# The second K/V unit's V issued before its K and the next query load, in a grouped-query attention kernel on one core

## Chip, core and metric

One core of one Trainium2 chip. The metric is the device time of the whole program in microseconds (us), lower is better.

## What is computed

```python
B, Hq, Hkv, Sq, Sk, D = 16, 32, 8, 288, 512, 128      # bf16
k, v = repeat(k, Hq // Hkv), repeat(v, Hq // Hkv)      # along the heads
p = softmax(einsum("bhqd,bhkd->bhqk", q, k) * D ** -0.5)
out = einsum("bhqk,bhkd->bhqd", p, v)
```

## The kernel before

There are 128 groups (one K/V head of one batch each), and three steps in a group, 384 in all. A step is three score matmuls of 128x512 on TensorE into PSUM, one exponential over 128x1536 on ScalarE, and twelve 128x129 products with V on TensorE; VectorE normalizes and evicts. In every sixth step VectorE computes 120 columns of the exponential itself (y_sb, t_sb, m_sb, e_sb, u_sb). I call it a shared step; a narrow 128x120 score matmul marks it. Steps 6, 12 and 18 are the first three.

K and V are loaded by units of four groups: K and Q by a transposing DMA, V by a plain one into vd_sb, all issued by SyncE in a fixed order. GpSimd copies V of one group at a time from vd_sb into v_sb. "Unit 1" is groups 4 to 7; K1 and V1 are its loads, Q4 is the query load of group 4. Step 12 is the first step of group 4.

```python
def op_v(u, eng=None, g0=0, g1=UG):                    # plain load, 512 KB for a unit
    ...
    eng.dma_start(vd_sb[:, sl, g0:g1], v_v[:, u * UG + g0:u * UG + g1]
                  ).then_inc(sem["us_v%d" % sl if u > 0 else "s_v%d" % g0], 16)

def op_s(n):                                           # scores of step n
    g, i = n // NC, n % NC                             # NC = 3 steps in a group
    waits = [have("k", g), have_q(g, i)]
    ...

def op_vc(g):                                          # V copy of group g, on GpSimd
    waits = [have("v", g)]
    if g >= 2:
        waits.append(("s_pv", NC * (g - 2) + 2))       # so many product groups are done
    ...

# the order of SyncE's issues is a sort by keys, in steps:
for u in range(1, NU):
    t = max(NC * UG * (u - NSLOT + 1) + 0.5, NC * (UG * u - 2.5) / AHEAD - 0.2)
    sp.append((t, lambda u=u: op_k(u)))
    sp.append((t + (2.0 if u >= NSLOT else 0.35), lambda u=u: op_v(u)))
for g in range(UG, NG):
    t = max(NC * (g - NQ + 1) + 1.2, NC * (g - 2.5) / AHEAD)
    sp.append((t, lambda g=g: op_q(g)))
...
sp.sort(key=lambda x: x[0])
```

## Time and profile before

| | before |
|---|---|
| median of 3 runs | 521.99 us (521.82 to 522.11) |
| traced run, span | 520.2 us |
| one step, steady | 1.330 us |
| K1, Q4, V1 landed | 18.0, 18.9, 21.9 us |
| score matmuls of step 12 start | 20.20 us |

A timeline line gives the start, the length, the engine, the source line, the operation, output and input, and, in square brackets, idle time of the engine before it and what ended that. A line of the DMA view gives the load, its issuing queue and the time from issue to landing, so a landing is the issue's start plus that number. Lines of the profile name source lines of the kernel: L449 is the score matmul, L460 the narrow one, L489 the product with V, L578 the V copy, L543 and L550 VectorE's t_sb and m_sb/e_sb.

### The profile page before, as it was taken

How to read it: one execution, taken by the hardware profiler on the slowest of the kernel's cores; microseconds unless marked ns; L12 is line 12 of the kernel's file. 1: busy time of each engine (PE TensorE's matmuls, PEld its weight loads, DVE VectorE, ACT ScalarE, POOL GpSimd, SP SyncE). 2: the span in 40 equal slices, each digit the busy share in tenths (PEclk: the TensorE clock that was granted, in tenths of full speed). 3: DMA queues.
4: the chain of work that ended last, by engine and by line, in shares of the span. 5: the costliest groups of instructions: out<-in, count | busy, mean ns of one | idle time of the engine just before them, and what ended most of it. 6: DMA issues, size and time to landing. Idle time of an engine off the chain costs nothing.

```text
span 520.2 us, 15366 instructions
## 1 busy us (share of the span) xinstructions
PE 516.2 (99%) x6226; PEld 394.6 (76%) x6226; DVE 370.5 (71%) x1322; ACT 513.4 (99%) x393; POOL 79.8 (15%) x135
## 2 busy tenths in 40 slices
PE   9999999999999999999999999999999999999997
PEld 5777777777777777777777777777777777777776
DVE  2767767777777677676776776767767767777777
ACT  7999999999999999999999999999999999999997
POOL 1111111111111111111111111111111111111110
PEclk9999999999999999999999999999999999999999
DMA  8999999899999998999999999999999999998212
GB/s 167 211 234 269 257 206 250 213 205 223 212 228 263 220 240 203 225 240 240 223 235 211 201 235 215 246 191 190 230 241 238 230 205 184 198 216 221 84 69 93
DMA packets 253782, 110.06 MB, mean 212 GB/s; under 512 B 220304, under 2 KB 237584, under 8 KB 253712
## 3 DMA queue, kind: packets, MB, share of 16 engines
q1 hardware_dynamic: 253568, 108.95, 99.5%
q8 instruction: 49, 0.80, 0.7%
q14 instruction: 21, 0.17, 0.1%
q10 hardware_dynamic: 144, 0.13, 0.1%
HBM read 16.91 MB, written 37.75 MB: 105 GB/s over the span
## 4 chain that ended last, share of the span: by engine, by line
PE 97%; DVE 2%; ACT 1%; issue 0%
PE ps_o L489 49%; PE ps_s L449 46%; PE ps_o L460 1%; ACT pt_sb L521 1%; ACT pt_sb L526 1%; PE ps_o L427 0%; DVE o_sb L595 0%; DVE u_sb L559 0%; DVE rl_sb L585 0%; DVE m_sb L550 0%; PE ps_s L427 0%; DVE pt_sb L566 0%; PE ps_o L414 0%; DVE t_sb L543 0%; DVE o_sb L605 0%
## 5 line engine op out<-in xcount | busy, mean ns | idle before, releaser
L526 ACT ACTIVATE pt_sb<-ps_s 128x1536 bf16<-128x1536 f32 (+2 forms) x384 | 508.2, 1438 | 0.1
L489 PE MATMUL ps_o<-v_sb,pt_sb 128*128 128x129 bf16 x4584 | 322.6, 220 | 0.1
L489 PEld LDWEIGHTS ps_o<-v_sb,pt_sb 128*128 128x128 bf16 x4584 | 282.6, 98 | 50.2 <-DVE o_sb L595 14.1
L449 PE MATMUL ps_s<-qt_sb,kt_sb 128*128 128x512 bf16 (+2 forms) x1536 | 308.9, 324 | 0.2
L595 DVE TENSOR_TENSOR o_sb<-ps_o,rl_sb 128x384 bf16<-128x384 f32 x382 | 211.7, 554 | 8.8
L449 PEld LDWEIGHTS ps_s<-qt_sb,kt_sb 128*128 128x128 bf16 x1536 | 123.6, 98 | 61.9 <-ACT pt_sb L526 0.7
L585 DVE RECIPROCAL rl_sb<-ps_o 128x3 f32<-128x3 f32 x382 | 67.8, 178 | 128.6 <-PE ps_o L489 127.2
L578 POOL COPY v_sb<-vd_sb 128x512 bf16<-128x512 bf16 x128 | 78.8, 616 | 429.2 <-PE ps_o L489 407.6
L559 DVE SCALAR_TENSOR_TENSOR u_sb<-u_sb,m_sb 128x120 f32<-128x120 f32 x128 | 36.2, 283 | 2.2
L566 DVE SCALAR_TENSOR_TENSOR pt_sb<-u_sb,e_sb 128x120 bf16<-128x120 f32 x64 | 18.1, 283 | 2.3
L559 DVE SCALAR_TENSOR_TENSOR u_sb<-m_sb 128x120 f32<-128x120 f32 x64 | 17.7, 276 | 0.0
L537 DVE TENSOR_SCALAR y_sb<-ps_o 128x120 f32<-128x120 f32 x64 | 16.2, 253 | 0.0
L550 DVE TENSOR_SCALAR m_sb<-t_sb 128x120 int32<-128x120 int32 x64 | 14.6, 228 | 2.2
L460 PE MATMUL ps_o<-qt_sb,kt_sb 128*128 128x120 bf16 x64 | 13.8, 216 | 0.0
L550 DVE TENSOR_SCALAR e_sb<-t_sb 128x120 int32<-128x120 int32 x64 | 13.8, 216 | 0.0
L543 DVE TENSOR_SCALAR t_sb<-y_sb 128x120 int32<-128x120 f32 x64 | 13.7, 214 | 0.0
L460 PEld LDWEIGHTS ps_o<-qt_sb,kt_sb 128*128 128x128 bf16 x64 | 6.3, 98 | 7.7 <-DVE o_sb L595 0.3
L521 ACT ACTIVATE pt_sb<-ps_s 128x512 bf16<-128x512 f32 (+1 forms) x6 | 4.3, 748 | 2.1 <-PE ps_s L449 2.1
L621 DVE TENSOR_REDUCE st_sb<-rl_sb 128x1 f32<-128x72 f32 (+1 forms) x16 | 3.4, 215 | 0.0
L623 DVE TENSOR_REDUCE st_sb<-rl_sb 128x1 f32<-128x72 f32 (+1 forms) x16 | 3.4, 215 | 0.0
L427 PE MATMUL ps_o<-const-bfloat16-1.0 128*128 128x512 bf16 (+1 forms) x6 | 2.4, 573 | 0.9 <-PEq L756 0.9
L685 ACT ACT_TABLE_LOAD x1 | 1.3, 1283 | 1.2 <-PEq L756 1.2
(32 smaller groups left out, 11.7 us busy)
## 6 DMA issues: line engine op xcount, KB each, us to landing
out_dram<-o_sb SPq DMA_DIRECT2D x126, 288.0 KB, 4.0
vd_sb<-in_v_dram SPq DMA_DIRECT2D x31, 512.0 KB, 5.4
qt_sb<-in_q_dram SPq DMA_TRANSPOSE x128, 5.1
out_dram<-o_sb SPq DMA_DIRECT2D x6, 96.0 KB, 1.8
kt_sb<-in_k_dram SPq DMA_TRANSPOSE x33, 5.1
vd_sb<-in_v_dram SPq DMA_DIRECT2D x2, 128.0 KB, 3.0
vd_sb<-in_v_dram SPq DMA_DIRECT2D x1, 256.0 KB, 3.5
kd_sb<-in_k_dram ACTq DMA_DIRECT2D x1, 128.0 KB, 2.3
```

Of the source, the lines that this page charges most:

```text
L449: ins = emit(eng, w_x, lambda: eng.matmul(ps_s[:, n % 2, c:c + w], kt_sb[:, sl, j, gi, :], qg[:, t * P:t * P + w], start=True, stop=True))
L460: emit(eng, [("s_ev", n - LAG - 1)], lambda: eng.matmul(ps_o[:, (n - LAG) % 2, BANK - W:BANK], kt_sb[:, (g // UG) % NSLOT, j, g % UG, :], ...
L489: ins = emit(eng, w_x, lambda: eng.matmul(outs(r)[:, t - r % NC * TPC, :], pt(g, t, j), v_sb[:, sl, gi * NJ + j, 0:DV], start=(x == 0), st ...
L526: emit(eng, waits, lambda: eng.activation(d, s, ACTF.Exp, scale=scale)).then_inc(sem["s_e"], 1)
L537: emit(eng, [("s_yb", nth(n) - NB), ("s_pv", n - LAG + 1)], lambda: eng.tensor_scalar(out=y_sb[:, b], in0=ps_o[:, (n - LAG) % 2, BANK - W: ...
L543: emit(eng, [("s_ym", 2 * (nth(n) - NB)), ("s_y", nth(n))], lambda: eng.tensor_scalar(out=t_sb[:, b], in0=y_sb[:, b], scalar1=Y_MUL, scala ...
L550: emit(eng, [("s_yp", nth(n) - NB), ("s_yb", nth(n))], lambda: eng.tensor_scalar(out=dst[:, b], in0=t_sb[:, b], scalar1=mask, scalar2=bits ...
L559: lambda: eng.scalar_tensor_tensor(out=u_sb[:, b, x], in0=src, scalar=QUARTIC[x], in1=m, op0=ALU.add, op1=ALU.mult)
L566: lambda: eng.scalar_tensor_tensor(out=pt_sb[:, n % NPT, CH - W:CH], in0=u_sb[:, b, 2], scalar=QUARTIC[3], in1=e_sb[:, b].bitcast(FP32), o ...
L578: emit(eng, waits, lambda: eng.tensor_copy(v_sb[:, sl, gi * NJ:(gi + 1) * NJ, 0:D], vd_sb[:, sl, gi].rearrange("p (j d) -> p j d", d=D))). ...
L585: emit(eng, [("s_pv", r + 1)], lambda: eng.reciprocal(rl_sb[:, TPC * r:TPC * (r + 1)].unsqueeze(2), outs(r)[:, :, D:DV])).then_inc(sem["s_ ...
L595: emit(eng, waits, lambda: eng.tensor_tensor(out=o_sb[:, g % NO, t0:t0 + TPC, :], in0=outs(r)[:, :, 0:D], in1=rl_sb[:, TPC * r:TPC * (r + ...
```

## The change

The intent: V of the second unit comes late (GpSimd waits 7.7 us for it), so it is asked for ahead of that unit's K and of the next query load. One sort key moves, and with it one issue; every engine but SyncE has the same instructions in the same order.

```diff
-            sp.append((t + (2.0 if u >= NSLOT else 0.35), lambda u=u: op_v(u)))
+            sp.append((t + (2.0 if u >= NSLOT else -0.05 if u == 1 else 0.35), lambda u=u: op_v(u)))
```

SyncE's order before is Q3, K1, Q4, V1, store 0, Q5; after, Q3, V1, K1, Q4, store 0, Q5.

## The prediction

> **What bounds the kernel now.** I read the page of the profiled execution first: its busy shares and its groups.
>
> ```profile
> span 520.2 us, 15366 instructions
> PE 516.2 (99%) x6226; PEld 394.6 (76%) x6226; DVE 370.5 (71%) x1322; ACT 513.4 (99%) x393; POOL 79.8 (15%) x135
> ...
> L526 ACT ACTIVATE pt_sb<-ps_s 128x1536 bf16<-128x1536 f32 (+2 forms) x384 | 508.2, 1438 | 0.1
> L489 PE MATMUL ps_o<-v_sb,pt_sb 128*128 128x129 bf16 x4584 | 322.6, 220 | 0.1
> ```
>
> TensorE and ScalarE are both busy 99% of the span, in lockstep: 384 steps, each of three 128x512 score matmuls, one exponential and twelve products with V. The chain of waits gives TensorE 97% of what ended last. The pace comes from the list of V copies on GpSimd, one per group of three steps: they start at 26.04 us (group 6) and at 509.00 us (group 127), so 482.96 us for 121 groups, 3.991 us a group, 1.330 us a step. The starts between go by the same 3.99 us (except one, at 34.50, whose V was late, and which moves none of those after it). So from 26 us on there is no slack that a load could give back; whatever a reordered load is worth must lie before 26 us. There, in the waits between 20 and 28 us, stand two that concern the moved transfer:
>
> ```profile
> POOL v_sb L578 <- DMA vd_sb<-in_v_dram: 7.7, 1, 7.7
> ...
> PEld ps_o L489 <- DVE o_sb L595: 0.6, 1, 0.6
> ```
>
> GpSimd waited 7.7 us for V from memory, and once the weight load of a product with V waited 0.6 us, the longest wait of its kind (the 62 of the whole run sum to 14.1 us). The chain in the same stretch (start, length, what) shows where it left TensorE:
>
> ```profile
> 21.02 0.69 PE ps_o L489 x12
> ...
> 22.08 0.47 DVE o_sb L595
> 22.55 0.23 DVE t_sb L543
> ...
> 22.80 0.52 DVE m_sb L550
> ...
> 25.12 0.85 PE ps_o L489 x12
> 25.97 0.65 PE ps_s L449 x3
> ```
>
> Between 21.71 and 25.12 us the end hangs on VectorE. The TensorE timeline has product groups starting at 22.18, 23.52, 25.12, 26.45 and 27.79 us: four intervals near 1.33 us except one, 23.52 to 25.12, which is 1.60. So 0.27 us is lost there. Why VectorE was late, by its own timeline (start, length) in this shared step and in the next one like it, eight microseconds later:
>
> ```profile
> 22.46 0.30 DVE L543 TENSOR_SCALAR t_sb<-y_sb 128x120 int32<-128x120 f32 x1
> 22.80 0.52 DVE L550 TENSOR_SCALAR m_sb<-t_sb 128x120 int32<-128x120 int32 x1
> ...
> 30.73 0.21 DVE L543 TENSOR_SCALAR t_sb<-y_sb 128x120 int32<-128x120 f32 x1
> 30.98 0.22 DVE L550 TENSOR_SCALAR m_sb<-t_sb 128x120 int32<-128x120 int32 x1
> ```
>
> The same instructions took 0.30 and 0.52 us instead of 0.21 and 0.22. GpSimd's timeline beside them:
>
> ```profile
> 22.07 1.17 POOL L578 COPY v_sb<-vd_sb 128x512 bf16<-128x512 bf16 x2 [7.68 <-DMA vd_sb<-in_v_dram]
> 26.04 0.62 POOL L578 COPY v_sb<-vd_sb 128x512 bf16<-128x512 bf16 x1 [2.79 <-PE ps_o L489]
> 30.03 0.62 POOL L578 COPY v_sb<-vd_sb 128x512 bf16<-128x512 bf16 x1 [3.38 <-PE ps_o L489]
> ```
>
> V of the second unit landed so late that the copies of groups 4 and 5 ran back to back, 22.07 to 23.24 us, across both slow instructions. Near 30 us one copy ran, 30.03 to 30.65, and VectorE's int32 work began at 30.73, just after it.
>
> **What the Trainium skill says.** "SBUF — State Buffer", the section with the two sides of SBUF and its diagram: VectorE and GpSimd share one port pair under an exclusive lock; a VectorE instruction in a 2-port mode, or with two SBUF inputs against a GpSimd read, and a GpSimd instruction exclude each other for a whole instruction. "VectorE: DVE Perf Modes", What auto-detection actually checks: the two-port mode needs a single source and the destination in SBUF. t_sb and m_sb are such; y_sb and the eviction, which read PSUM, are not. The trace agrees: the first end near the copies' ends, the others keep their 0.25 and 0.55 us beside a copy. "DMA: Bandwidth & Descriptors", Queues, rings and completion order: on each DMA engine descriptors are consumed in ring order. The landings below agree: they come in the order of issue.
>
> **The change part by part.** Nothing is added or removed; one issue moves. For the unit u=1 the sort key of V goes from 4.32 to 3.92, below K's 3.97 and Q4's 4.17. Old order on SyncE: K1, Q4, V1, store 0; new: V1, K1, Q4, store 0. No other key changes. The SyncE timeline has K1 issued at 11.21 us (3.28 long), Q4 at 14.53 (2.53), V1 at 17.10 (0.58), and no semaphore waits among them. The transfers' times from issue to landing, from the DMA view cut to each issue:
>
> ```profile
> kt_sb<-in_k_dram SPq DMA_TRANSPOSE x1, 6.8
> ...
> qt_sb<-in_q_dram SPq DMA_TRANSPOSE x1, 4.4
> ...
> vd_sb<-in_v_dram SPq DMA_DIRECT2D x1, 512.0 KB, 4.8
> ```
>
> So K1 landed at 18.0, Q4 at 18.9, V1 at 21.9 us.
>
> (a) Gain. V1 is issued at 11.2 and lands, with its own 4.8 us, near 16 us. Group 4's copy is then released by the program's other wait (eight product groups done), near 17.76 us, where VectorE has no shared work; group 5's by eleven groups done, 0.03 us after the reciprocal at 21.73 as at 30.03 after 30.00: near 21.76, over at 22.38, before t_sb at 22.46. VectorE's stretch from y_sb to the eviction then takes 32.40 - 30.10 = 2.30 us instead of 24.51 - 21.83 = 2.68: 0.38 us sooner, of which some 0.11 is slack in front of TensorE (in the later step the eviction ends at 32.95 and, at 1.33 a step, the products come near 33.11, with 0.05 for the signal). Left on the path: 0.38 - 0.11 = 0.27 us, the same as the lost interval. Both ways agree.
>
> (b) Cost. K1 and Q4 now lie behind V1. Who needs them: the narrow score matmul marks every sixth step (12.75, 20.80, 29.07 us), so the step with 20.80 is step 12, the first of unit 1, and its score matmuls start at 20.20. K1 had 2.2 us to spare there and Q4 1.3. What pushes them: on SyncE one issue of 0.6 us; in the DMA engines 524 kB, at the 370 GB/s that the slices from 20 to 22 us show (364 and 374), 1.4 us (an estimate). Q4 then lands between 19.5 and 20.3; if V1 takes the 3.0 us that it took behind Q4, at 21.9. So the wait of step 12 is most likely 0 to 0.3 us, at worst near 1.7. Q5, issued after all three in either order at 18.28, landed at 23.8 and is needed at 24.20: its queue position is unchanged.
>
> Sum: -0.27 plus an expected +0.1 to +0.2, on 521.99: about 521.8.
>
> **The rivals.** First, K1 and Q4 become the new wait: for it, Q4's spare 1.3 us is about V1's 1.4 us, and V1's first packets may meet a slow stretch (the slices from 15 to 17 us moved only 65 and 91 GB/s). It would give 522 to 523.4 us. Against it, that stretch of idle DMA also means the engines were not full, so V1 may be absorbed. Second, TensorE's lost 0.27 us is not on the path because ScalarE sets the pace: then nothing changes, 522.0. For it, ScalarE is shown without idle time; against it, after 25.12 us TensorE keeps 1.33 us and does not catch up. Third, the late V is worth far more than the collision, as its 7.7 us wait suggests: then 514 us. Against it, GpSimd is 15% busy, and group 4's copy ended near 22.65, before its first product at 23.52; nobody waited for it directly. I give that almost nothing.
>
> **Range and chances.** The runs before spread 521.82 to 522.11. A clean gain gives 521.72, and the noise takes that to 521.4; with a wait of step 12 the time goes to 522.8. Range 521.3 to 522.8. Two per cent is 10.4 us; no term here reaches a fifth of it: within 2% is 0.98.
>
> **What would show it.** Right: GpSimd's copies of groups 4 and 5 come singly near 17.8 and 21.8 us; t_sb and m_sb of step 12 take 0.21 and 0.22 us; no 1.60 interval near 25 us; the copy of group 6 starts near 25.8 instead of 26.04 and all later ones keep that lead. Wrong: a wait of a score load for kt_sb or qt_sb near 20.2 us, with a shift of the copies to later; or the copies earlier and the end unmoved. What would make it wrong altogether is a slow transpose behind V1, which the trace of before cannot show.

## The result

| | before | after |
|---|---|---|
| median | 521.9 us (521.82 to 522.11, 6 runs) | 522.17 us (521.9 to 522.72, 6 runs) |
| ratio | | 1.0006, 95% interval 0.9993 to 1.0019 |
| traced run | 521.84 us | 521.9 us |

The ratio is the mean time of the fast runs of one kernel over that of the other's of the same rounds, so it is not quite the ratio of the medians quoted. Within the interval the two are the same. But the changed kernel's runs lie wider apart, and upwards.

The trace of after answers the prediction's own list. First VectorE's timeline of step 12, then GpSimd's:

```profile
22.81 0.21 DVE L543 TENSOR_SCALAR t_sb<-y_sb 128x120 int32<-128x120 f32 x1
23.06 0.22 DVE L550 TENSOR_SCALAR m_sb<-t_sb 128x120 int32<-128x120 int32 x1
```

```profile
18.11 0.62 POOL L578 COPY v_sb<-vd_sb 128x512 bf16<-128x512 bf16 x1 [3.37 <-PE ps_o L489]
22.11 0.62 POOL L578 COPY v_sb<-vd_sb 128x512 bf16<-128x512 bf16 x1 [3.38 <-PE ps_o L489]
26.10 0.62 POOL L578 COPY v_sb<-vd_sb 128x512 bf16<-128x512 bf16 x1 [3.37 <-PE ps_o L489]
```

The two copies come singly, released by TensorE and no longer by the DMA; the two VectorE instructions are back to 0.21 and 0.22 us from 0.30 and 0.52, and the product groups start at 23.86 and 25.19 us, 1.33 apart. The collision is gone, as predicted. Yet the copy of group 6 starts at 26.10 us and not at 25.8: the whole run was 0.35 us later before any of this (VectorE's fifth reciprocal, one of which opens each step's normalizing, starts at 14.10 us instead of 13.75). So I judge the stretch of each trace that begins after that start and ends with the last V copy: 509.00 - 13.75 = 495.25 us before, 509.06 - 14.10 = 494.96 after. Inside that stretch this trace gained 0.29 us.

The other side of the bargain is in the landings, from the DMA view cut to each issue (V1 issued at 11.04, K1 at 11.66, Q4 at 15.85 us):

```profile
vd_sb<-in_v_dram SPq DMA_DIRECT2D x1, 512.0 KB, 5.0
...
kt_sb<-in_k_dram SPq DMA_TRANSPOSE x1, 7.7
...
qt_sb<-in_q_dram SPq DMA_TRANSPOSE x1, 4.4
```

V1 landed at 16.0, K1 at 19.4 and Q4 at 20.25 us; step 12's scores started at 20.55. Without the late start of this run they would have started near 20.2, before Q4 was there. This trace is a lucky one, and the next experiment shows the others.

### The profile page after: what moved, and what is told of

The parts are those of the page before. It is cut to its first block, busy times and chain, and to the rows that moved or that the text cites. A ratio compares the mean times of both kernels' runs of the same rounds, so it can differ in the third digit from the quotient of the medians.

```text
span 520.2 us, 15260 instructions
## 1 busy us (share of the span) xinstructions
PE 510.7 (98%) x6120; PEld 394.7 (76%) x6226; DVE 370.4 (71%) x1322; ACT 513.3 (99%) x393; POOL 79.8 (15%) x135
## 4 chain that ended last, share of the span: by engine, by line
PE 96%; issue 1%; ACT 1%; DVE 1%; DMA 0%
PE ps_o L489 50%; PE ps_s L449 45%; PE ps_o L460 1%; ACT pt_sb L521 1%; ACT pt_sb L526 1%; DMA kd_sb<-in_k_dram 0%; DVE o_sb L595 0%; DVE u_sb L559 0%; DVE rl_sb L585 0%; PE ps_s L427 0%; PE ps_o L414 0%; DVE o_sb L605 0%; DVE pt_sb L566 0%; PE ps_o L677 0%; DVE t_sb L543 0%
## 5 line engine op out<-in xcount | busy, mean ns | idle before, releaser
L449 PE MATMUL ps_s<-qt_sb,kt_sb 128*128 128x512 bf16 (+2 forms) x1430 | 290.1, 320 | 4.7
L578 POOL COPY v_sb<-vd_sb 128x512 bf16<-128x512 bf16 x128 | 78.9, 616 | 429.2 <-PE ps_o L489 413.7
L550 DVE TENSOR_SCALAR m_sb<-t_sb 128x120 int32<-128x120 int32 x64 | 14.3, 223 | 2.2
```

Of the source, the lines that this page charges most:

```text
L449: ins = emit(eng, w_x, lambda: eng.matmul(ps_s[:, n % 2, c:c + w], kt_sb[:, sl, j, gi, :], qg[:, t * P:t * P + w], start=True, stop=True))
L550: emit(eng, [("s_yp", nth(n) - NB), ("s_yb", nth(n))], lambda: eng.tensor_scalar(out=dst[:, b], in0=t_sb[:, b], scalar1=mask, scalar2=bits ...
L578: emit(eng, waits, lambda: eng.tensor_copy(v_sb[:, sl, gi * NJ:(gi + 1) * NJ, 0:D], vd_sb[:, sl, gi].rearrange("p (j d) -> p j d", d=D))). ...
```

## The experiments

The theory to test: the change removes a collision that costs up to 0.27 us, and puts K1 and Q4, needed at step 12, behind 512 KB; how late they land differs from run to run. Rivals: the order does not touch the time; V's late landing, and not the collision, slows that step; a wait at step 12 is made up later. The table collects the traces of all runs. "Stretch" is as above; "above" is what exceeds 494.95 us, the shortest seen; the last column is what the intervals between TensorE's product groups show above 1.33 us.

| trace | V1 landed | Q4 landed | 5th reciprocal | stretch | above | seen on TensorE |
|---|---|---|---|---|---|---|
| before | 21.9 | 18.9 | 13.75 | 495.25 | 0.30 | collision 0.27 |
| e5_before | 20.85 | 18.7 | 13.79 | 494.96 | 0.01 | none |
| e2_hold5 | 20.8 | 18.6 | 14.20 | 494.95 | 0 | none |
| e8_warm6 | 21.8 | 19.1 | 14.09 | 494.96 | 0.01 | none |
| e9_before_collide | 23.0 | 19.3 | 13.91 | 495.53 | 0.58 | V late 0.36, collision 0.21 |
| after | 16.0 | 20.25 | 14.10 | 494.96 | 0.01 | none |
| e1_after | 17.5 | 21.05 | 14.03 | 495.59 | 0.64 | step 12 0.63 |
| e11_after_again | 17.2 | 21.4 | 14.11 | 495.84 | 0.89 | step 12 0.88 |
| e3_collide | 17.1 | 21.3 | 14.16 | 495.96 | 1.01 | step 12 0.77, collision 0.22 |
| e4_two_v | 17.6 | 22.6 | 13.76 | 497.41 | 2.46 | step 12 2.45 |
| e7_split | 14.4 (group 4) | 19.0 | 14.11 | 494.95 | 0 | none |
| e10_split_again | 15.2 (group 4) | 19.45 | 13.98 | 494.96 | 0.01 | none |

In every row the lost intervals before 27 us account for the whole stretch to within 0.03 us. Nothing that is lost there is made up in the 480 us that follow.

### e1_after and e11_after_again: the changed kernel again

No edit.

> The changed kernel again, unaltered, for more runs and a second trace. Theory (the collision's 0.27 us is gained, and a wait of step 12 for Q4 gives a part of it back from run to run): 521.6 to 522.5 us, mean within 0.3 us of before, scattered more than before; in the trace Q4 lands within 0.3 us of the start of step 12's score matmuls, before or after. Rival (the order does not touch the time): the same mean and the same scatter as before, Q4 well ahead of step 12.

> The changed kernel a third time, traced beside the split one. Theory (its loss is the wait of step 12, where Q4 lands between 20.2 and 21.3 us against a need of 20.2 to 20.55): in the trace, what the stretch from the fifth reciprocal to the last V copy is above 494.95 us equals the wait at step 12 within 0.1 us, and Q4's landing less the undisturbed start of step 12 gives that wait; median 0.3 to 0.6 us above before. Rival: the stretch is longer without such a wait, or the wait is there without the stretch being longer.

Measured: e1_after 522.31 us (522.04 to 522.59) against 521.8 before, ratio 1.0008 (0.9994 to 1.0022); its mean lies 0.44 us above before's, where at most 0.3 was expected. e11_after_again 522.74 us (521.59 to 522.89) against 521.84, ratio 1.0009 (0.9995 to 1.0022): 0.90 us above by the medians, 0.53 by the means, with 0.3 to 0.6 expected. Its five runs fall in two groups, 521.59 and 521.95 against 522.74 to 522.89, so the median says less than the mean. TensorE's timeline of e11_after_again:

```profile
19.88 0.84 PE L489 MATMUL ps_o<-v_sb,pt_sb 128*128 128x129 bf16 x12
21.43 0.77 PE L449 MATMUL ps_s<-qt_sb,kt_sb 128*128 128x512 bf16 x3 [0.71 <-DMA qt_sb<-in_q_dram]
22.04 0.22 PE L460 MATMUL ps_o<-qt_sb,kt_sb 128*128 128x120 bf16 x1
```

The narrow matmul says that this is step 12. Its scores waited for Q4, which landed at 21.4 us (issued 16.99, 4.4 us), and the next product group came at 22.09 us, 2.21 us after the last instead of 1.33. The wait of 0.88 us and the stretch's 0.89 us agree, as the theory had put down. In e1_after the same wait makes 0.63 of 0.64 us; "within 0.3 us of the start" failed there by size: without the wait, step 12 would have started near 20.48 us, and Q4 landed at 21.05. The unchanged-time rival falls. Over the three sessions the changed kernel's 16 runs have a mean of 522.31 us and the 24 runs of before in the same rounds 521.88: 0.43 us, and by session 0.32, 0.44 and 0.53 (the scatter of the 40 runs gives this difference a standard error of about 0.1 us, if they are independent). Each interval alone holds 1; the three agree in sign with what the traces show.

### e2_hold5: the collision taken away, the old order kept

```diff
-                waits.append(("s_pv", NC * (g - 2) + 2))
+                waits.append(("s_pv", NC * (g - 2) + (4 if g == UG + 1 else 2)))
```

> The kernel before, its transfers in the old order, but the V copy of group 5 held until thirteen product groups are done instead of eleven, so that it cannot run back to back with group 4's. Theory (the 0.27 us lost near 25 us come of the copies' collision with VectorE's int32 work): m_sb of step 12 back to 0.22 us, t_sb still up to 0.30, the 1.60 us interval back to at most 1.38, the run 0.2 to 0.3 us under before: about 521.6. Rival (V's late landing, or the DMA traffic, is what slows that step): m_sb stays at 0.5 us, interval 1.60, time as before, 521.9.

Measured: 521.88 us (521.7 to 522.06) against 521.8, ratio 1.0000 (0.9986 to 1.0014). The expected 0.2 to 0.3 us did not appear. m_sb took 0.22 us, but the trace decides nothing on the cause: here V1 landed at 20.8 us instead of 21.9, and group 4's copy ran from 20.89 to 21.5, so group 5's would not have been pushed even without the hold. What it did show is that the collision is not in every run of the old order, which the first trace could not tell. The case that this run missed, V late and the copies apart, came by chance in e8_warm6, below.

### e5_before: the kernel before, traced again

No edit.

> The kernel before, unaltered, for a second trace. In the first trace V1 landed at 21.9 us; in the run with group 5's copy held, whose transfers have the same order, it landed at 20.8. Theory (the collision is there only when V1 lands after about 21.2 us, so that group 4's copy pushes group 5's into VectorE's int32 work): if V1 lands before 21.2 here, m_sb takes 0.22 us and no 1.60 us interval is near 25 us; if after, both are back. No wait of step 12 for Q4 in either case. Rival (the collision is in every run of this order): the interval is there whatever V1's landing. Time 521.6 to 522.1.

Measured: 521.67 us (521.53 to 521.93) against 521.6. GpSimd's timeline and VectorE's m_sb:

```profile
20.98 0.62 POOL L578 COPY v_sb<-vd_sb 128x512 bf16<-128x512 bf16 x1 [6.25 <-DMA vd_sb<-in_v_dram]
21.80 0.61 POOL L578 COPY v_sb<-vd_sb 128x512 bf16<-128x512 bf16 x1 [0.21 <-PE ps_o L489]
```

```profile
22.75 0.22 DVE L550 TENSOR_SCALAR m_sb<-t_sb 128x120 int32<-128x120 int32 x1
```

V1 landed at 20.85 us, the copies did not touch, and the stretch is 494.96 us, as short as the changed kernel's best. V was waited for 6.2 us and that cost nothing. So the gain that I predicted is there to be had only in those runs in which V1 lands later than about 21.2 us. (An estimate: in the first trace the pushed copy ended 1.3 us after V1's landing, and t_sb starts near 22.5 us; in a run that starts later the limit is later by as much.) Of the five traces with the old order it landed at 20.8, 20.85, 21.8, 21.9 and 23.0.

### e3_collide: the collision forced, V early

```diff
-                waits.append(("s_pv", NC * (g - 2) + 2))
+                waits.append(("s_pv", NC * (g - 2) + (5 if g == UG else 2)))
```

on the changed kernel.

> The changed kernel, V early, but the V copy of group 4 held until eleven product groups are done, so that the copies of groups 4 and 5 again run back to back beside VectorE's shared step. Theory (collision): t_sb of step 12 begins or ends only when the second copy ends, some 0.4 us later, and an interval of 1.55 to 1.75 us is back near 25 us; about 0.3 us above the changed kernel. Rival (V's late landing or its traffic): no such interval, time as the changed kernel.

Measured: 522.22 us (522.05 to 523.71) against 521.8, ratio 1.0013 (0.9999 to 1.0026). By the medians it is no slower than e1_after of the same session, and by the means 0.32 us slower (522.61 against 522.29), which hangs on two runs, 522.98 and 523.71; so the 0.3 us expected above that kernel are not resolved. The trace resolves them. GpSimd's timeline, then VectorE's, then TensorE's:

```profile
22.94 1.17 POOL L578 COPY v_sb<-vd_sb 128x512 bf16<-128x512 bf16 x2 [8.14 <-PE ps_o L489]
```

```profile
23.64 0.54 DVE L543 TENSOR_SCALAR t_sb<-y_sb 128x120 int32<-128x120 f32 x1
24.22 0.22 DVE L550 TENSOR_SCALAR m_sb<-t_sb 128x120 int32<-128x120 int32 x1
```

```profile
24.69 0.84 PE L489 MATMUL ps_o<-v_sb,pt_sb 128*128 128x129 bf16 x12
...
26.24 0.85 PE L489 MATMUL ps_o<-v_sb,pt_sb 128*128 128x129 bf16 x12
```

V1 landed at 17.1 us, the two copies ran back to back from 22.94 to 24.11, and t_sb ended at 24.18, just behind them; the product groups that follow are 24.69 and 26.24 us, 1.55 apart. So the stretched VectorE instructions come from the copies and not from V's landing or its traffic. That is what "SBUF — State Buffer", SBUF: two separate sides, of the Trainium skill says of the port pair that the two engines share, and here 0.21 us became 0.54. The wait at step 12, 0.77 us, is in this trace too.

### e9_before_collide: the collision forced, old order

The same edit on the kernel before.

> The kernel before, old order, but the V copy of group 4 held until eleven product groups are done, so that it runs back to back with group 5's in every run, whenever V1 lands. Theory (a collision costs about 0.25 us on the path): an interval of 1.5 to 1.65 us near 25 us, and the median 0.15 to 0.3 us above the kernel before of the same chip. Rival (ScalarE sets the pace, or the lost time is made up): interval or not, the same median as before within 0.1 us.

Measured: 521.91 us (521.8 to 522.26) against 521.6, ratio 1.0002 (0.9988 to 1.0016). The medians are 0.31 us apart, the means of the same rounds (521.95 and 521.73) 0.22: what the theory expects, but inside the noise. The traced run, 522.26 us, is the slowest, and shows something that I had ruled out. The chain of waits (start, length, what):

```profile
17.22 5.80 DMA vd_sb<-in_v_dram
...
23.14 0.76 POOL v_sb L578
...
24.03 0.84 PE ps_o L489 x12
```

V1 landed only at 23.0 us, 1.1 us later than the first trace had it and after the time at which the hold would have let the copy go. So the hold played no part in this trace. The product of group 4 itself waited for the copy (1.69 us after the one before), and the copies then ran beside VectorE's u_sb instructions, two of which took 1.18 us together instead of 0.60 (the next product group came after 1.54 us). The old order thus has its own late runs.

### e4_two_v: twice the bytes ahead of K1 and Q4

```diff
-... -0.05 if u == 1 else 0.35
+... -0.05 if u == 1 else -11.155 if u == 2 else 0.35
```

V of the third unit, too, goes ahead of K1.

> The changed kernel with V of the third unit, too, ahead of K1 and Q4: another 512 KB in front of them. Theory (K1 and Q4 have little room left): Q4 lands some 1.3 us later than in the changed kernel, near 21.5 us, and step 12's score matmuls wait for it by about 1.0 to 1.3 us; the run ends 0.8 to 1.2 us above the changed kernel. Rival (loads have room or a wait there is made up later): no wait, or a wait that the end does not show, time within 0.2 us of the changed kernel.

Measured: 523.91 us (523.64 to 524.46) against 521.8, ratio 1.0041 (1.0027 to 1.0055), the one clear difference. TensorE's timeline at step 12:

```profile
22.65 0.77 PE L449 MATMUL ps_s<-qt_sb,kt_sb 128*128 128x512 bf16 x3 [2.28 <-DMA qt_sb<-in_q_dram]
```

The interval between product groups was 3.78 us, so 2.45 us were lost; the median is 2.1 us over before. That Q4 behind more bytes makes step 12 wait is confirmed, and the rival falls. The size was under-estimated: I expected a wait of 1.0 to 1.3 us. SyncE's timeline shows why: K1's issue took 6.70 us (from 12.19), and Q4, next in line, was issued at 18.93, just before V of the third unit landed at 19.0.

### e7_split and e10_split_again: only group 4's quarter ahead

```diff
+            if u == 1:
+                sp.append((t - 0.05, lambda u=u: op_v(u, None, 0, 1)))
-            sp.append((t + (2.0 if u >= NSLOT else 0.35), lambda u=u: op_v(u)))
+            sp.append((t + (2.0 if u >= NSLOT else 0.35), lambda u=u: op_v(u, None, 1 if u == 1 else 0, UG)))
```

with a semaphore of its own for that quarter, and the hold of e2_hold5.

> The kernel before with only group 4's quarter of V1 (128 KB) ahead of K1 and Q4, the other three groups where V1 was, and group 5's copy held until thirteen product groups are done. Theory (what the change gives back is Q4 pushed by V1's 512 KB): a quarter of the bytes pushes Q4 by 0.3 to 0.7 us, it lands near 19.5, step 12 does not wait, there is no collision: 0.3 to 0.6 us under the changed kernel, at or up to 0.3 under before, 521.5 to 521.9. Rival (any transfer put ahead of K1 costs step 12 the same): an interval of 1.5 us or more at step 12, about 522.2.

> The split kernel again (group 4's quarter of V1 ahead of K1 and Q4, the rest behind, group 5's copy held), beside the changed kernel on one chip. Theory: in the trace neither a wait of step 12 nor a stretched m_sb, 494.9 to 495.0 us from the fifth reciprocal to the last V copy, and a median 0.3 to 0.7 us under the changed kernel's, 0 to 0.3 under before's. Rival (the earlier lead was chance): the changed kernel's median within 0.15 us.

Measured: 521.49 us (521.37 to 521.84) against 521.6, ratio 0.9995 (0.9981 to 1.0009); again, 521.76 us (521.37 to 521.94) against 521.84, ratio 0.9997 (0.9983 to 1.001). In the second session the changed kernel, on the same chip, had 522.74: 0.98 us more by the medians, 0.69 by the means, with 0.3 to 0.7 expected. GpSimd's timeline of e10_split_again (the added lines move L578 to L580):

```profile
18.00 0.61 POOL L580 COPY v_sb<-vd_sb 128x512 bf16<-128x512 bf16 x1 [3.38 <-PE ps_o L491]
24.66 0.61 POOL L580 COPY v_sb<-vd_sb 128x512 bf16<-128x512 bf16 x1 [6.04 <-PE ps_o L491]
```

Group 4's copy comes at its earliest time, group 5's after the shared work, Q4 lands at 19.0 and 19.45 us, and both stretches are at the shortest, 494.95 and 494.96. A quarter of the bytes ahead of K1 costs step 12 nothing, so it is the amount and not the mere place that matters. The hold went with the quarter in both runs; the quarter without it was not run. Both ratios lie under 1 and both intervals hold 1: by the traces it has neither loss, by the clock it is at best 0.16 us ahead of before (mean of 10 runs, 521.64, over 18 of before, 521.80), which this study does not prove.

### e8_warm6: the start of the run

```diff
-    WARM = 5
+    WARM = 6
```

with the hold of e2_hold5.

> The kernel before with group 5's copy held as in the earlier run, and one more 128x512 warm-up matmul ahead of the first transposes. In the traces so far the first twelve score matmuls took 2.45 us in some and 3.12 to 3.34 us in others, which set the fifth product group 0.3 to 0.45 us apart before any transfer of this study. Theory (a start scatter of TensorE, not the order of transfers, makes runs of one kernel differ): with less idle time before the transposes the first scores take 2.45 us in the trace and the five times lie closer together, about 521.5 to 521.9. Rival: the start is not changed by it, or the added matmul of some 0.4 us is simply in the way: 521.9 to 522.3.

Measured: 521.85 us (521.33 to 522.06) against 521.6, ratio 1.0000 (0.9987 to 1.0014). The first twelve scores took 2.66 us, the fifth reciprocal came at 14.09, and the five times lie no closer together. The attempt failed. That the starts differ is in the table (13.75 to 14.20 us, before any transfer moved is needed); what sets them stays open. This scatter of 0.45 us is as large as the effects under study, and is why the medians alone could not decide them.

But its trace is the test that e2_hold5 missed. GpSimd's timeline, then VectorE's:

```profile
21.93 0.61 POOL L578 COPY v_sb<-vd_sb 128x512 bf16<-128x512 bf16 x1 [7.20 <-DMA vd_sb<-in_v_dram]
```

```profile
23.05 0.22 DVE L550 TENSOR_SCALAR m_sb<-t_sb 128x120 int32<-128x120 int32 x1
```

V1 landed at 21.8 us, late enough that group 5's copy, due near 22.1, would have run from 22.54 to about 23.1 beside t_sb (from 22.80; an estimate). Held until 24.76 it did not: t_sb and m_sb took 0.21 and 0.22 us, and the stretch is 494.96 us. A wait of 7.2 us for V, with the copies apart, cost nothing in the old order. It is one trace, and its start was 0.34 us later than the first one's.

## Why the prediction was right or wrong

The time, 522.17 us, fell inside the range, and "within 2%" held; but the range took in a clean gain as well as a loss, so that is weak support. The text leaned to a gain, to 521.8 us, and what came was a loss. By its own steps:

- **Bound and place: right.** The steady pace of the steps sets the end (which of the two engines at 99%, TensorE or ScalarE, sets that pace was not tested), and all differences lie before 27 us and last to the end, in all twelve traces.
- **Gain, (a): right in mechanism, size and place for the trace it was read from; wrong as an expectation.** The 0.27 us came of the collision: forced with V early, it was back at 0.22 us. But the text took one trace for every run. In e5_before, with the same instructions, the loss was 0.01 us. The term -0.27 should have been multiplied by how often V1 lands late, which one trace does not tell.
- **Cost, (b): right in what would wait, wrong in how Q4 is pushed, and so too small.** The text put Q4's landing between 19.5 and 20.3 us, "most likely 0 to 0.3 us" of wait, at worst 1.7. It landed at 20.25, 21.05, 21.3 and 21.4 us in the four traces with this order, and the waits were 0, 0.63, 0.77 and 0.88. The failed term is "on SyncE one issue of 0.6 us". SyncE's timeline of before, then of e11_after_again:

```profile
11.21 3.28 SPq L293 DMA_TRANSPOSE kt_sb<-in_k_dram  x1
14.53 2.53 SPq L313 DMA_TRANSPOSE qt_sb<-in_q_dram  x1
```

```profile
11.97 4.98 SPq L293 DMA_TRANSPOSE kt_sb<-in_k_dram  x1
16.99 2.47 SPq L313 DMA_TRANSPOSE qt_sb<-in_q_dram  x1
```

SyncE's issue of K1 was itself lengthened, from 2.9 to 3.3 us in the old order to 4.1 to 5.1 behind V1, and Q4 cannot be issued until it ends. So Q4 was issued at 16.7 us (mean of four traces) instead of 14.2 (mean of five), 2.5 us later and not 0.6. The 1.4 us of bytes do not show after that: Q4's own time from issue to landing was 4.3 us instead of 4.7. It landed at 21.0 us instead of 18.9, 2.1 later. In all twelve traces K1's issue ended 0.1 to 0.7 us before the load directly ahead of it landed: Q3 at 14.3 to 14.8 us in the old order, V1 at 16.1 to 17.5 in the changed one, group 4's quarter at 14.4 and 15.1 in the split, V of the third unit at 19.0 in e4_two_v. Why a transposing issue lasts that long was not tested.
- **Sum: sign wrong.** -0.27 plus 0.1 to 0.2 leaned to a small gain. With the waits measured (mean 0.57) and the old order's losses (0.30 and 0.01 in its two unedited traces), the traces give about +0.4 us; with e9_before_collide and e2_hold5 counted too (0.58 and 0, the hold played no part in either), about +0.35. The runs give 0.32 to 0.53.
- **Rivals.** The first, K1 and Q4 as the new wait, with 522 to 523.4 us, is what happened. The second, that ScalarE hides a loss of TensorE, is refuted by the table. The third, that V's late landing matters directly, got "almost nothing"; as a gain of 8 us it is indeed nothing, but e9_before_collide shows a run in which V landed at 23.0 us and cost 0.36 us directly.
- **Two misread lines.** "That stretch of idle DMA" was not all idle: the same view gives the DMA engines a busy share of 2.14 from 15 to 16 us, at 65 GB/s, and 0.43 from 16 to 17. And y_sb was hardly beside a copy in the first trace (it ended at 22.08 us, the copies began at 22.07); the trace of after has it beside one (22.18 to 22.43, the copy from 22.11 to 22.73), where it kept its 0.25 us.

Left open: how often V1 lands late in the old order (five traces are few), why K1's issue lasts until the load ahead of it has nearly landed, and what differs between the starts of runs.

## What to carry to other kernels

In a queue that is served in order, moving one load ahead delays all that it passes, so list for each passed load when it lands and when it is first needed. List also what an issue itself may wait for: here the issue of K1 behind V1 held up Q4. V1 had room until about 21.2 us and K1 and Q4 only until 20.2, so the old order was by deadline, and a long wait on an engine that is 15% busy (7.7 us of GpSimd) was no reason to change it. If only part of a load is needed early, move that part alone (here, in two traces, this took away both losses; a gain in time was not shown). And where effects are tenths of a microsecond, read two or three traces of the same kernel before believing in a stall, and compare a stretch that leaves out the start.

## What the Trainium skill lacked or had wrong

- "DMA: Bandwidth & Descriptors", Issuing engines are not separate DMA queues, calls the sequencer's time to initiate a DMA "usually small relative to the DMA itself". For the transposing loads here it is not: K1's issue held SyncE for 4.14 us of 7.7 us to landing in the changed kernel's first trace, 4.98 of 8.5 in e11_after_again and 6.70 of 9.3 in e4_two_v, and 2.5 to 3.3 us in the runs with no plain load or only 128 KB directly ahead. No page that I read tells that the issue stretches with the plain bytes queued ahead; in the twelve traces it ended 0.1 to 0.7 us before the load ahead landed.
- The same page, Queues, rings and completion order, gives the order in which descriptors are consumed, but not the scatter of landings. With unchanged order, V1 took 4.6 to 5.8 us from issue and landed between 20.8 and 23.0 us.
- "SBUF — State Buffer", SBUF: two separate sides, was found neither lacking nor wrong. It says that whichever of the two instructions starts first gets the pair for the whole instruction, and the other fully blocks. In e3_collide t_sb (from 23.64 us) started after the second of the two copies (23.50), took 0.54 us and ended just behind it; in the first trace it started during the first copy (22.46), took 0.30 us and ended (22.76) just behind that one. Both fit.
